# Splitting float64 weights into two float32r parts: a 24-bit conversion of five VectorE operations and one subtraction, in place of eight VectorE and two GpSimd operations

## The chip, the cores and the metric

The kernel runs on one core of one Trainium2 chip. The metric is device time in microseconds (us) of one execution. The core has a matmul engine (TensorE, PE in the profile, its weight loads PEld), VectorE (DVE), ScalarE (ACT), GpSimd (POOL) and SyncE (SP), which here issues all DMA transfers. Each engine works through its own list of instructions in order and waits only where an operand or a buffer is not ready.

## The reference

Clustered attention, then two feed-forward layers on its output:

```python
# attention: B, H, S, D = 2, 8, 768, 64; a key counts only in the query's cluster (16 clusters)
mask = q_assign[:, :, :, None] == k_assign[:, :, None, :]
scores = np.where(mask, scale * np.matmul(q, k.transpose(0, 1, 3, 2)), -1e9)
attn_out = np.matmul(softmax(scores), v)
x = attn_out.transpose(0, 2, 1, 3).reshape(B * S, H * D)      # 1536 x 512
# first layer: w_in 512 x 2048 and w_out 2048 x 512 are float64
r = np.maximum(x @ w_in, 0.0)
x = (r * r) @ w_out
# second layer: 4 experts, w1 512 x 1024 and w2 1024 x 512 each, float32
for e in range(4):
    out += p[:, e:e + 1] * (np.maximum(x @ w1[e], 0.0) @ w2[e])
```

`scale * (1 / sqrt(...))` makes the first layer's two weight matrices float64; every other input is float32.

## The kernel before, in words

A float32 value is carried as hi + lo, two float32r parts, so that three single-pass products (hi hi, hi lo, lo hi) add up to a float32 product. Every weight therefore has to be split on the chip into a hi and a lo tile before PE can use it.

**Attention** is a software pipeline over 96 units of 128 queries, a step each. `ORDER` writes out in which order the parts of an even and of an odd step are emitted: scores (`S`), row maximum on DVE (`M`, line 507), exponential on ACT (`E`, line 518), transposes (`T0`, `T1`) whose hi part ACT copies (`H`, line 536) and whose lo part DVE subtracts (`L`, line 537), products with v (`P`, lines 545 and 547) and their sum (`O`, line 563). The part `K`, in even steps from step 8 on, pops one item of the list `cq`: the conversion of the four blocks of the first layer's first weight chunk, and behind it the two loads of that chunk's `w_out` half.

**The first MoE layer** has 4 chunks of 512 hidden units, the second 8. Its work is a list `its` of (chunk, token block of 512, group of 128 hidden units), 12 per chunk. In slot n the program emits `gemm1(n)` (12 matmuls of 512 columns, lines 637 to 639), `gemm2(n - 4)` (12 matmuls, line 667) and then `run_plan(n)`, which emits what is due of weight loads and conversions. After `gemm1` of the first layer ACT runs relu, square and a copy to the hi part (lines 645 to 647, "the trio" below), and GpSimd subtracts for the lo part `hl` (line 648). After every fourth `gemm2` four accumulators `o` are emptied: by ACT copies for the first chunk (line 678), by DVE additions after it (line 680).

**The conversion** of a block (128 hidden units, a 128x512 tile) is `split64`. A float64 arrives as two 32-bit words. Before, it had three stages, a slot apart: shift and mask the high word (`f1` to `f4`, lines 153 to 169) and multiply by a 0/1 mask on GpSimd (line 170); copy to hi on ACT (line 174) and extract the remaining mantissa bits (lines 175 to 183, the subtraction on GpSimd); subtract hi (line 187) and add the remaining bits (line 190). `split_plan` puts the stages on slots, one block per slot: slots 0 to 19 and 24 to 31 start a block each (28 blocks), 4 more are converted in attention. `split32`, for the second layer, has one stage.

The scheduling is manual: each engine's order is the order in which the program is written.

Of the kernel before, what the change touches and what calls it, by code (L numbers as in the profile page):

```python
# [8 lines left out]
F32 = mybir.dt.float32  # L9
F32R = mybir.dt.float32r  # L10
I32 = mybir.dt.int32
AF = mybir.ActivationFunctionType
ALU = mybir.AluOpType
AX = mybir.AxisListType
PSUM = bass.MemoryType.PSUM

# A float32 value is carried as hi + lo, two float32r parts of 12 significant
# bits each, so that single-pass products of the parts add up to the float32
# product.  Inside an attention head, token p * 6 + t sits in column t * 128 + p.


# Order of the parts of a step of the attention pipeline, and the steps, counted
# from the first one of a head, at which its preparation is done.
ORDER = [
# [3 lines left out]
START = {'t': [1, 3, 3, 3], 'stack1': 6, 'stack': 7, 'head': [[1, 2, 3], [7, 8, 8]]}  # L28
FL = {"f7": "P", "chain": "V", "po": "V", "xh": "P", "xm": "P", "xl": "P", "kh": "P", "kl": "P", "vh": "P", "vl": "P", "f4": "V"}
AT = {"gap": 3, "stack1": -11, "stack": -9, "assign": -9, "oh0": -5, "oh1": -4, "splitv": -3,  # L30
# [4 lines left out]
def moe_attention_kernel(  # L35
# [13 lines left out]
    nc = tc.nc  # L49

    def eng(x):
        return {"V": nc.vector, "P": nc.gpsimd}[FL[x]]

# [8 lines left out]
    FC = 512  # L62
# [5 lines left out]
    scale = 1.0 / float(D) ** 0.5  # L68
# [17 lines left out]

# [1 line left out]
    # The first layer's weights are float64: a pair of 32-bit words each, the  # L88
    # upper one with the sign, the exponent and 20 mantissa bits.
    NC1 = moe_w_in.shape[1] // FC  # L90
# [33 lines left out]
    def w_block(ci, part, j):  # L124
        """hi and lo of the 128 hidden units j of a chunk: [128, 4, 128] or [128, 512]"""
        if (ci, part) not in w_t:
            w_t[ci, part] = tuple(
                w_pool[ci % 2, part].tile([128, 4, 512], F32R, tag=f"w{part}{x}", name=f"w{part}{x}")
                for x in "hl")
        hi, lo = w_t[ci, part]  # L130
        if part == 0:
            return hi[:, :, j * 128:(j + 1) * 128], lo[:, :, j * 128:(j + 1) * 128]
        return hi[:, j], lo[:, j]

    def split64(ci, part, j, cv):
        r = raw_t[ci, part, j // 2].bitcast(I32)
        jj = j % 2
        if part == 0:
            shp = [128, 4, 128]
            r = r.rearrange("p (k f w) -> p k f w", k=4, w=2)[:, :, jj * 128:(jj + 1) * 128]  # L140
            low, high = r[:, :, :, 0], r[:, :, :, 1]
        else:
            shp = [128, 512]
            r = r.rearrange("p (k f w) -> p k f w", k=2, w=2)[:, jj]
            low, high = r[:, :, 0], r[:, :, 1]
        st = {}

        def tile_(x):
            st[x] = cv.tile(shp, F32, tag="cv" + x, name="cv" + x)
            return st[x]  # L150

        def f1():
            nc.vector.tensor_scalar(  # L153
                tile_("a").bitcast(I32), high, 3, 0x3FFFFFF8,
                op0=ALU.logical_shift_left, op1=ALU.bitwise_and)

        def f2():
            nc.vector.tensor_scalar(  # L158
                tile_("b").bitcast(I32), high, 0x78000000, None, op0=ALU.bitwise_and)

        def f3():
            ai = st["a"].bitcast(I32)
            nc.vector.scalar_tensor_tensor(  # L163
                out=ai, in0=high, scalar=-0x40000000, in1=ai,
                op0=ALU.bitwise_and, op1=ALU.bitwise_or)

        def f4():
            e = eng("f4") if cv is cv_p[0] and len(cv_p) == 1 else nc.vector
            e.tensor_scalar(st["b"], st["b"], 2.0 ** -15, None, op0=ALU.is_ge)  # L169
            nc.gpsimd.tensor_tensor(st["a"], st["a"], st["b"], op=ALU.mult)  # L170

        def f5():
            st["hi"], st["lo"] = w_block(ci, part, j)
            nc.scalar.copy(st["hi"], st["a"])
            nc.vector.tensor_scalar(  # L175
                tile_("c").bitcast(I32), st["a"].bitcast(I32), -0x800000, None,
                op0=ALU.bitwise_and)

        def f6():
            nc.vector.scalar_tensor_tensor(  # L180
                out=tile_("d").bitcast(I32), in0=low, scalar=9, in1=st["c"].bitcast(I32),
                op0=ALU.logical_shift_right, op1=ALU.bitwise_or)
            nc.gpsimd.tensor_tensor(st["d"], st["d"], st["c"], op=ALU.subtract)

        def f7():
            e = eng("f7") if cv is cv_p[0] and len(cv_p) == 1 else nc.vector
            e.tensor_tensor(st["b"], st["a"], st["hi"].bitcast(F32), op=ALU.subtract)  # L187

        def f8():
            nc.vector.scalar_tensor_tensor(  # L190
                out=st["lo"], in0=st["d"], scalar=2.0 ** -20, in1=st["b"],
                op0=ALU.mult, op1=ALU.add)
        return [[f1, f2, f3, f4], [f5, f6], [f7, f8]]

# [10 lines left out]
    def split_plan(ci, part, j, slot):  # L205
        """the stages of a block, a slot apart: [(slot, order, f)]"""
        st = []

        def stage(k):
            if k == 0:  # L210
                st.extend((split64 if ci < NC1 else split32)(ci, part, j, cv_p[j % len(cv_p)]))
            for f in st[k]:
                f()
        return [(slot + k, -k, lambda k=k: stage(k)) for k in range(3 if ci < NC1 else 1)]

    # ================= attention =================
    with tc.manual_schedule():
# [22 lines left out]
        def load_pair(j):  # L240
            """k and q of heads 2j and 2j + 1, side by side"""
            b, h = divmod(2 * j, H)
# [20 lines left out]

# [1 line left out]
        c_sb = sm_p.tile([128, D], F32, tag="c_sb", name="c_sb", bufs=1)  # L265
# [13 lines left out]
        for c in range(C):  # L279
            nc.gpsimd.memset(wgt[:, :, c:c + 1], float(C - c))  # L280
        # sel[4 t + 2 h + s, t, 64 h + d] = 1: adds up 1 / sum (hi and lo) of a
        # token for the 64 rows of its head
        idv = identf[0:NTT * 4, 0:NTT * 4].rearrange("p (t h s) -> p t h s", t=NTT, h=2)
# [5 lines left out]

# [1 line left out]
        # q carries the softmax scale, a power of two, from here on.  # L291
        # Stacked along the contraction: [q hi; q hi] with [k hi; k lo], then
        # [q lo; one-hot cluster] with [k hi; -2^100 off its cluster], whose last
        # rows add 0 inside a cluster and -2^100 outside.
        vt, stk, kq, ohs, ohm = {}, {}, {}, {}, {}
# [14 lines left out]
        def double(i, nm):  # L310
            """k or q of a head, twice side by side"""
            t = nat[i, nm] = nat_p.tile([128, NTT, 2, D], F32, tag=nm, name=nm)
# [16 lines left out]
        def split_direct(i, nm, m):  # L329
            """the stacks of head i from its transposes on both partition halves"""  # L330
            def new(x, rows):
# [28 lines left out]
        def trans_slot(j, nm, half):  # L360
            """transpose k or q of a head pair and split it"""
            def f():
# [110 lines left out]
        def onehot_first():  # L473
            """the one-hot rows of head 0, without a detour over DMA"""
            for e, nm in ((1, "k2"), (0, "q2")):
# [11 lines left out]

# [1 line left out]
        s_ps, p_sb, nb_t, sums_t, pt_t, po_t, xs_t = {}, {}, {}, {}, {}, {}, {}  # L489
# [133 lines left out]

# [1 line left out]
        mp = {}  # L625
# [94 lines left out]

# [1 line left out]
        def warm_pe(n):  # L722
            """products of no use, that keep the clock of TensorE up"""
            w = ps_o.tile([128, 256], F32, tag="po", name="po")
# [10 lines left out]

# [1 line left out]
        csq = sm_p.tile([128, D], F32, tag="csq", name="csq", bufs=1)  # L737
# [69 lines left out]

        # what a step does besides its unit of queries
        early, slots = {}, {}
# [87 lines left out]

        # the last pair of units and the last heads, beside the first products of the MoE
        def early_gemm1(n):
# [22 lines left out]

# [1 line left out]
        dpv = dp.rearrange("p b t e -> p (b t) e")  # L924
# [7 lines left out]

# [1 line left out]
        for nm in ("w10", "w11", "acc"):  # L934
# [43 lines left out]
```

## Time and profile before

| | |
|---|---|
| median of 3 runs | 1134.59 us (1133.72, 1134.59, 1138.93) |
| profiled execution, from first to last instruction | 1132.6 us |
| PE busy | 1079.9 us (95%) |
| DVE busy | 618.4 us (55%) |
| ACT busy | 439.6 us (39%) |
| POOL busy | 397.9 us (35%) |
| PE mean granted clock | 0.980 |

The profiled execution is an execution of its own; its record gives the span, and the three runs lie 1.1, 2.0 and 6.3 us above that span. Busy times overlap, since the engines work side by side. A matmul's shown duration includes the pipeline's depth (0.39 us for one of 512 columns), so PE's pace is read from the distance between starts, or from the number of matmuls in a stretch of time. "Idle before" an instruction is the time its engine stood still ahead of it, and the arrow names what it waited for.

### The profile page before, as it was taken

The numbers are of one execution on the slowest core, as the hardware profiler recorded it, in microseconds if no ns is written. First come the engines' busy times: TensorE is split into PE (matmuls) and PEld (weight loads), VectorE is DVE, ScalarE is ACT, GpSimd is POOL, SyncE is SP. The second block draws the span as 40 slices with busy tenths as digits, with TensorE's granted clock in tenths as the row PEclk, the third lists the DMA queues.
The fourth block names the chain that finished last, engine by engine and source line by source line (L and its number), as shares of the span: only waits on it lengthen the run. The fifth ranks groups of instructions, "written<-read, shape, count | busy, mean of one in ns | idle before, by whom it ended". The sixth has DMA issues, their size and how long they took to land.

```text
span 1132.6 us, 14354 instructions
## 1 busy us (share of the span) xinstructions
PE 1079.9 (95%) x5502; PEld 910.1 (80%) x5502; DVE 618.4 (55%) x1014; ACT 439.6 (39%) x894; POOL 397.9 (35%) x364
## 2 busy tenths in 40 slices
PE   8799999999988887989999999999999999999998
PEld 7798888888866666878888888888888888888887
DVE  7799999999799999695012223223222222322322
ACT  5578887888733333333443112111111111111110
POOL 3346755553366666555445212020211102021000
PEclk9899999999998988999999999999999999999999
DMA  4565555663022221121110201011110201100011
GB/s 146 131 153 129 127 121 126 144 173 77 1 74 75 75 75 65 46 66 47 38 38 1 75 1 65 11 38 38 38 38 1 75 1 38 38 1 1 1 38 74
DMA packets 51812, 70.61 MB, mean 62 GB/s; under 512 B 25664, under 2 KB 28224, under 8 KB 51744
## 3 DMA queue, kind: packets, MB, share of 16 engines
q1 hardware_dynamic: 51744, 69.70, 21.9%
q8 instruction: 43, 0.70, 0.3%
q14 instruction: 25, 0.20, 0.1%
HBM read 43.05 MB, written 3.15 MB: 41 GB/s over the span
## 4 chain that ended last, share of the span: by engine, by line
PE 58%; DVE 14%; issue 0%; DVEq 0%
PE o L667 29%; PE h L637 9%; PE h L638 9%; PE h L639 9%; DVE cvb L158 3%; DVE cvc L175 2%; DVE w0l L190 2%; DVE cvd L180 1%; DVE cvb L187 1%; DVE w1l L190 1%; DVE cva L163 1%; DVE cva L153 1%; DVE cvb L169 1%; DVE acc L680 0%; DVE acc L692 0%
## 5 line engine op out<-in xcount | busy, mean ns | idle before, releaser
L651 DVE SCALAR_TENSOR_TENSOR hl<-h,hh 128x512 fp32r<-128x512 f32 x96 | 66.4, 692 | 393.4 <-ACT hh L650 393.4
L650 ACT ACTIVATE hh<-h 128x512 fp32r<-128x512 f32 x96 | 57.4, 598 | 429.0 <-PE h L639 429.0
L637 PE MATMUL h<-xh,w0h 128*128 128x512 f32 x560 | 218.4, 390 | 0.0
L638 PE MATMUL h<-xl,w0h 128*128 128x512 f32 x560 | 218.0, 389 | 0.0
L639 PE MATMUL h<-xh,w0l 128*128 128x512 f32 x560 | 217.9, 389 | 0.0
L667 PE MATMUL o<-w1h,hh 128*128 128x512 f32 x384 | 149.4, 389 | 0.0
L667 PE MATMUL o<-w1l,hh 128*128 128x512 f32 x384 | 149.4, 389 | 0.0
L667 PE MATMUL o<-w1h,hl 128*128 128x512 f32 x384 | 149.4, 389 | 0.0
L202 POOL TENSOR_TENSOR w0l<-raw,w0h 128x512 fp32r<-128x512 f32 x32 | 41.2, 1289 | 236.7 <-ACT w0h L201 236.7
L637 PEld LDWEIGHTS h<-xh,w0h 128*128 128x128 f32 x560 | 105.6, 189 | 22.0
L638 PEld LDWEIGHTS h<-xl,w0h 128*128 128x128 f32 x560 | 105.4, 188 | 22.1
L639 PEld LDWEIGHTS h<-xh,w0l 128*128 128x128 f32 x560 | 105.4, 188 | 21.9
L537 DVE TENSOR_TENSOR ptl<-t,pth 128x384 fp32r<-128x384 f32 x192 | 99.8, 548 | 8.4 <-ACT pth L536 7.7
L667 PE MATMUL o<-hh,w1h 128*128 128x512 f32 x192 | 79.9, 416 | 24.2 <-ACT acc L678 13.3
L531 PE MATMUL t<-identf,p 128*128 128x128 f32 x576 | 92.9, 284 | 7.4 <-DVE ptl L537 6.6
L507 DVE TENSOR_REDUCE nb<-s 128x1 f32<-128x768 f32 x96 | 91.0, 948 | 7.4 <-PE s L498 6.6
L536 ACT CAST pth<-t 128x384 fp32r<-128x384 f32 x192 | 83.9, 479 | 28.0 <-PE t L531 26.7
L648 POOL TENSOR_TENSOR hl<-r,hh 128x512 fp32r<-128x512 f32 x48 | 71.3, 1487 | 65.8 <-ACT hh L647 28.9
L518 ACT ACTIVATE p<-s,nb 128x768 f32<-128x768 f32 x96 | 86.7, 903 | 6.9 <-DVE nb L507 6.0
L498 PE MATMUL s<-k,q 80*128 80x384 f32 (+1 forms) x384 | 86.5, 347 | 0.2 <-DVE q L340 0.2
L667 PE MATMUL o<-hh,w1l 128*128 128x512 f32 x192 | 79.5, 414 | 5.0 <-DVE w1l L190 5.0
L667 PEld LDWEIGHTS o<-w1h,hh 128*128 128x128 f32 x384 | 72.1, 188 | 15.0
(147 smaller groups left out, 1842.2 us busy)
## 6 DMA issues: line engine op xcount, KB each, us to landing
raw<-in_moe_w_dram SPq DMA_DIRECT2D x16, 1024.0 KB, 5.0
raw<-in_moe_w_in_dram SPq DMA_DIRECT2D x8, 1024.0 KB, 5.2
raw<-in_moe_w_out_dram SPq DMA_DIRECT2D x8, 1024.0 KB, 4.9
q<-nqh SPq DMA_DIRECT2D x42, 192.0 KB, 3.0
k<-nkh SPq DMA_DIRECT2D x28, 192.0 KB, 3.7
q<-nql SPq DMA_DIRECT2D x28, 192.0 KB, 3.8
nv<-in_v_dram SPq DMA_DIRECT2D x16, 192.0 KB, 3.8
out_dram<-acc SPq DMA_DIRECT2D x12, 256.0 KB, 2.1
```

Of the source, the lines that this page charges most:

```text
L498: nc.tensor.matmul(s[:, j, 0:HALF], stk[i, nq][:, t * 128:(t + 1) * 128], stk[i, nk][:, j * HALF:(j + 1) * HALF], start=first, stop=not first)
L507: nc.vector.tensor_reduce(out=nb, in_=s_ps[u][:, :, 0:HALF], axis=AX.XY, op=ALU.max, negate=True)
L518: nc.scalar.activation(p, s_ps.pop(u)[:, :, 0:HALF], AF.Exp, bias=nb_t.pop(u), accum_out=sums_t[hp][:, i % 2, t:t + 1])
L531: nc.tensor.transpose(tp[:, j], p_sb[u][:, half, j * 128:(j + 1) * 128], identf)
L536: return (lambda: nc.scalar.copy(dh, tp), lambda: nc.vector.tensor_tensor(dl, tp, dh.bitcast(F32), op=ALU.subtract))
L537: lambda: nc.vector.tensor_tensor(dl, tp, dh.bitcast(F32), op=ALU.subtract))
L637: nc.tensor.matmul(ps, wh[:, kt, ms], xh[tb][:, kt], start=(kt == 0), stop=False)
L638: nc.tensor.matmul(ps, wh[:, kt, ms], xl[tb][:, kt], start=False, stop=False)
L639: nc.tensor.matmul(ps, wl[:, kt, ms], xh[tb][:, kt], start=False, stop=(kt == KD - 1))
L648: nc.gpsimd.tensor_tensor(hl, r, hh.bitcast(F32), op=ALU.subtract)
L651: nc.vector.scalar_tensor_tensor(out=hl, in0=ps, scalar=0.0, in1=hh.bitcast(F32), op0=ALU.max, op1=ALU.subtract)
L667: nc.tensor.matmul(o_t[n], a, b, start=(ft == 0 and z == 0), stop=(ft == NF - 1 and z == 2))
```

## The change

`split64` gets two stages. The first, on DVE alone, clears the sign of the high word, raises the value to at least 2^-15 (read as float32, in place of the 0/1 mask and its product), shifts, puts sign and top exponent bit back and adds three bits of the low word, so that one 32-bit float with 24 significant bits is left in `a`. The second copies `a` to hi on ACT and subtracts hi from `a`: on GpSimd while attention runs (`len(cv_p) == 1`), on DVE after it. The tiles `cvb`, `cvc` and `cvd` are gone. The list `cq` holds 3 items a block instead of 8, so attention's conversion is emitted in steps 8 to 34 instead of 8 to 74, and the two `w_out` loads come in steps 32 and 34 instead of 72 and 74.

```diff
-FL = {"f7": "P", "chain": "V", ..., "f4": "V"}
+FL = {"chain": "V", ...}
...
         def f1():
+            a = st["a"] = cv.tile(shp, F32, tag="cva", name="cva")
             nc.vector.tensor_scalar(
-                tile_("a").bitcast(I32), high, 3, 0x3FFFFFF8,
+                a.bitcast(I32), high, 0x7FFFFFFF, None, op0=ALU.bitwise_and)
+            nc.vector.tensor_scalar(a, a, 2.0 ** -15, None, op0=ALU.max)
+            nc.vector.tensor_scalar(
+                a.bitcast(I32), a.bitcast(I32), 3, 0x3FFFFFF8,
                 op0=ALU.logical_shift_left, op1=ALU.bitwise_and)
 
         def f2():
-            nc.vector.tensor_scalar(
-                tile_("b").bitcast(I32), high, 0x78000000, None, op0=ALU.bitwise_and)
-
-        def f3():
             ai = st["a"].bitcast(I32)
             nc.vector.scalar_tensor_tensor(
                 out=ai, in0=high, scalar=-0x40000000, in1=ai,
                 op0=ALU.bitwise_and, op1=ALU.bitwise_or)
-
-        def f4():
-            e = eng("f4") if cv is cv_p[0] and len(cv_p) == 1 else nc.vector
-            e.tensor_scalar(st["b"], st["b"], 2.0 ** -15, None, op0=ALU.is_ge)
-            nc.gpsimd.tensor_tensor(st["a"], st["a"], st["b"], op=ALU.mult)
-
-        def f5():
-            st["hi"], st["lo"] = w_block(ci, part, j)
-            nc.scalar.copy(st["hi"], st["a"])
-            nc.vector.tensor_scalar(
-                tile_("c").bitcast(I32), st["a"].bitcast(I32), -0x800000, None,
-                op0=ALU.bitwise_and)
-
-        def f6():
             nc.vector.scalar_tensor_tensor(
-                out=tile_("d").bitcast(I32), in0=low, scalar=9, in1=st["c"].bitcast(I32),
+                out=ai, in0=low, scalar=29, in1=ai,
                 op0=ALU.logical_shift_right, op1=ALU.bitwise_or)
-            nc.gpsimd.tensor_tensor(st["d"], st["d"], st["c"], op=ALU.subtract)
-
-        def f7():
-            e = eng("f7") if cv is cv_p[0] and len(cv_p) == 1 else nc.vector
-            e.tensor_tensor(st["b"], st["a"], st["hi"].bitcast(F32), op=ALU.subtract)
-
-        def f8():
-            nc.vector.scalar_tensor_tensor(
-                out=st["lo"], in0=st["d"], scalar=2.0 ** -20, in1=st["b"],
-                op0=ALU.mult, op1=ALU.add)
-        return [[f1, f2, f3, f4], [f5, f6], [f7, f8]]
+
+        def f3():
+            hi, lo = w_block(ci, part, j)
+            nc.scalar.copy(hi, st["a"])
+            e = nc.gpsimd if len(cv_p) == 1 else nc.vector
+            e.tensor_tensor(lo, st["a"], hi.bitcast(F32), op=ALU.subtract)
+        return [[f1, f2], [f3]]
...
-        return [(slot + k, -k, lambda k=k: stage(k)) for k in range(3 if ci < NC1 else 1)]
+        return [(slot + k, -k, lambda k=k: stage(k)) for k in range(2 if ci < NC1 else 1)]
```

The change's short description also speaks of the lo part of the squared relu tiles (`hl`) on VectorE; in the code that subtraction is the same GpSimd instruction in both kernels, line 648 before and line 629 after.

The order in which DVE has its instructions in the MoE slots, where a block of the first layer's weights is converted per slot (`w1l` is a lo tile of `w_out`). Before, one block after the other:

```order
496 L190 SCALAR_TENSOR_TENSOR w1l<-cvd,cvb 128x512
497 L175 TENSOR_SCALAR cvc<-cva 128x512
498 L180 SCALAR_TENSOR_TENSOR cvd<-raw,cvc 128x512
499 L153 TENSOR_SCALAR cva<-raw 128x512
500 L158 TENSOR_SCALAR cvb<-raw 128x512
501 L163 SCALAR_TENSOR_TENSOR cva<-raw,cva 128x512
502 L169 TENSOR_SCALAR cvb<-cvb 128x512
503 L187 TENSOR_TENSOR cvb<-cva,w1h 128x512
```

And after the change:

```order
488 L173 TENSOR_TENSOR w1l<-cva,w1h 128x512
489 L153 TENSOR_SCALAR cva<-raw 128x512
490 L155 TENSOR_SCALAR cva<-cva 128x512
491 L156 TENSOR_SCALAR cva<-cva 128x512
492 L162 SCALAR_TENSOR_TENSOR cva<-raw,cva 128x512
493 L165 SCALAR_TENSOR_TENSOR cva<-raw,cva 128x512
```

Eight instructions of a block, taken from three blocks in turn, became six, of which the five on `cva` are of one block and each read what the one before wrote.

GpSimd in the same slots, before (`hl` is the lo part of a squared relu tile):

```order
184 L183 TENSOR_TENSOR cvd<-cvd,cvc 128x512
185 L170 TENSOR_TENSOR cva<-cva,cvb 128x512
186 L648 TENSOR_TENSOR hl<-r,hh 128x512
187 L183 TENSOR_TENSOR cvd<-cvd,cvc 128x512
188 L170 TENSOR_TENSOR cva<-cva,cvb 128x512
```

And after the change, from the last instructions of attention (`rb`, `xh`, `xl` are its normalized outputs) to the second layer's first lo tile `w0l`:

```order
159 L584 TENSOR_TENSOR rb<-rb,xs 128x384
160 L596 TENSOR_TENSOR xh_79<-rb,zeros 128x384
161 L598 TENSOR_TENSOR xl_82<-rb,xh_79 128x384
162 L629 TENSOR_TENSOR hl<-r,hh 128x512 x37
163 L183 TENSOR_TENSOR w0l<-raw,w0h 128x4x128
```

Of three GpSimd instructions a slot one is left.

DVE in attention, at the step in which the conversion begins (`nb` is the row maximum of a unit, `ptl` the lo part of its transposes). Before:

```order
72 L537 TENSOR_TENSOR ptl<-t,pth 128x3x128 x2
73 L153 TENSOR_SCALAR cva<-raw 128x512
74 L507 TENSOR_REDUCE nb<-s 128x1
75 L409 TENSOR_REDUCE A<-m 128x192
76 L439 TENSOR_REDUCE mx<-A 128x12
```

And after the change:

```order
72 L518 TENSOR_TENSOR ptl<-t,pth 128x3x128 x2
73 L153 TENSOR_SCALAR cva<-raw 128x512
74 L155 TENSOR_SCALAR cva<-cva 128x512
75 L156 TENSOR_SCALAR cva<-cva 128x512
76 L488 TENSOR_REDUCE nb<-s 128x1
```

The row maximum now comes behind three operations of the conversion instead of one.

## Rows read from the trace of the kernel before

**Rows 1.** The overview, the span in 40 equal slices of 28.3 us: busy tenths of PE and of DVE.

```profile
PE   8799999999988887989999999999999999999998
...
DVE  7799999999799999695012223223222222322322
```

**Rows 2.** Windows, from 315 to 515 us and from 520 to 1120 us: length, busy us and number of instructions of PE, PEld, DVE, ACT and POOL, then the granted clock, the DMA share and GB/s.

```profile
315.00:515.00 200.00, 170.78 (x692) 137.36 (x691) 183.95 (x227) 73.24 (x125) 121.65 (x82) 0.92 0.21 69
520.00:1120.00 600.00, 600.00 (x2649) 496.99 (x2648) 143.48 (x212) 123.16 (x215) 117.95 (x92) 1.00 0.09 30
```

**Rows 3.** The waits of PE: who waited for what, us in total, how often, the longest.

```profile
PE o L667 <- ACT acc L678: 13.3, 3, 4.9
PE o L667 <- DVE acc L680: 10.9, 2, 7.1
...
PE o L667 <- DVE w1l L190: 5.0, 4, 2.4
```

**Rows 4.** Timeline of PE: start, duration, instruction, and in brackets the idle time before it and its releaser. A matmul that waited for the first block's `w1l`, and two behind a wait for an accumulator.

```profile
317.39 0.50 PE L667 MATMUL o<-hh,w1l 128*128 128x512 f32 x1 [1.87 <-DVE w1l L190]
...
406.71 0.63 PE L667 MATMUL o<-hh,w1l 128*128 128x512 f32 x1
407.13 0.63 PE L667 MATMUL o<-hl,w1h 128*128 128x512 f32 x1
```

**Rows 5.** Timeline of DVE over one slot, with the same columns.

```profile
359.17 1.59 DVE L190 SCALAR_TENSOR_TENSOR w0l<-cvd,cvb 128x512 fp32r<-128x512 f32 x1
360.69 1.52 DVE L175 TENSOR_SCALAR cvc<-cva 128x512 int32<-128x512 int32 x1
362.25 0.69 DVE L180 SCALAR_TENSOR_TENSOR cvd<-raw,cvc 128x512 int32<-128x512 int32 x1
362.85 0.42 DVE L153 TENSOR_SCALAR cva<-raw 128x512 int32<-128x512 int32 x1
363.19 1.52 DVE L158 TENSOR_SCALAR cvb<-raw 128x512 int32<-128x512 int32 x1
364.63 0.68 DVE L163 SCALAR_TENSOR_TENSOR cva<-raw,cva 128x512 int32<-128x512 int32 x1
365.24 0.41 DVE L169 TENSOR_SCALAR cvb<-cvb 128x512 f32<-128x512 f32 x1
365.57 0.68 DVE L187 TENSOR_TENSOR cvb<-cva,w0h 128x512 f32<-128x512 f32 x1
366.35 1.59 DVE L190 SCALAR_TENSOR_TENSOR w0l<-cvd,cvb 128x512 fp32r<-128x512 f32 x1
```

**Rows 6.** Timeline of POOL over the same slot.

```profile
358.61 1.60 POOL L170 TENSOR_TENSOR cva<-cva,cvb 128x512 f32<-128x512 f32 x1 [1.37 <-DVE cvb L169]
360.18 1.75 POOL L648 TENSOR_TENSOR hl<-r,hh 128x512 fp32r<-128x512 f32 x1
363.08 1.35 POOL L183 TENSOR_TENSOR cvd<-cvd,cvc 128x512 f32<-128x512 f32 x1 [1.16 <-DVE cvd L180]
```

**Rows 7.** Timeline of ACT over the same slot: the hi copy of a block, then the trio.

```profile
360.25 0.62 ACT L174 CAST w0h<-cva 128x512 fp32r<-128x512 f32 x1 [4.74 <-POOL cva L170]
360.78 0.59 ACT L645 ACTIVATE r<-h 128x512 f32<-128x512 f32 x1
361.40 0.64 ACT L646 ACTIVATE r<-r 128x512 f32<-128x512 f32 x1
362.07 0.62 ACT L647 CAST hh<-r 128x512 fp32r<-128x512 f32 x1
```

**Rows 8.** Groups of instructions by line and shape over the whole span: count, busy us, mean ns of one, idle us before and its releasers. The accumulator additions of the first layer.

```profile
L680 DVE TENSOR_TENSOR acc<-o,acc 128x512 f32<-128x512 f32 x36 | 23.7, 687 | 65.5 <-PE o L667 65.4
```

**Rows 9.** The same view of DVE from 50 to 240 us, the stretch of attention in which the first half of the first chunk is converted.

```profile
L163 DVE SCALAR_TENSOR_TENSOR cva<-raw,cva 128x512 int32<-128x512 int32 x4 | 2.7, 681 | 0.0
L190 DVE SCALAR_TENSOR_TENSOR w0l<-cvd,cvb 128x512 fp32r<-128x512 f32 x4 | 2.7, 663 | 0.0
L180 DVE SCALAR_TENSOR_TENSOR cvd<-raw,cvc 128x512 int32<-128x512 int32 x4 | 2.7, 663 | 0.0
...
L175 DVE TENSOR_SCALAR cvc<-cva 128x512 int32<-128x512 int32 x4 | 2.3, 565 | 0.0
L158 DVE TENSOR_SCALAR cvb<-raw 128x512 int32<-128x512 int32 x4 | 2.2, 560 | 0.0
L153 DVE TENSOR_SCALAR cva<-raw 128x512 int32<-128x512 int32 x4 | 1.7, 415 | 0.0
L169 DVE TENSOR_SCALAR cvb<-cvb 128x512 f32<-128x512 f32 x4 | 1.5, 387 | 0.0
```

**Rows 10.** The window of that stretch, columns as in Rows 2.

```profile
50.00:240.00 190.00, 181.84 (x1332) 163.35 (x1332) 181.04 (x365) 151.44 (x356) 111.01 (x119) 0.98 0.57 135
```

**Rows 11.** Timeline of DVE at the end of attention (columns as in Rows 4).

```profile
299.65 0.42 DVE L153 TENSOR_SCALAR cva<-raw 128x512 int32<-128x512 int32 x1
299.99 0.42 DVE L158 TENSOR_SCALAR cvb<-raw 128x512 int32<-128x512 int32 x1
...
303.28 0.43 DVE L563 TENSOR_TENSOR xs<-po,tmp 64x256 f32<-64x256 f32 x1 [1.93 <-ACT tmp L561]
...
310.73 0.56 DVE L617 TENSOR_TENSOR xl<-rb,xh 128x384 fp32r<-128x384 f32 x1 [0.58 <-ACT xh L613]
311.21 0.42 DVE L175 TENSOR_SCALAR cvc<-cva 128x512 int32<-128x512 int32 x1
```

More of the change, by code (lines that the diff above doesn't have):

```diff
@@ L28 @@
 START = {'t': [1, 3, 3, 3], 'stack1': 6, 'stack': 7, 'head': [[1, 2, 3], [7, 8, 8]]}
-FL = {"f7": "P", "chain": "V", "po": "V", "xh": "P", "xm": "P", "xl": "P", "kh": "P", "kl": "P", "vh": "P", "vl": "P", "f4": "V"}
+FL = {"chain": "V", "po": "V", "xh": "P", "xm": "P", "xl": "P", "kh": "P", "kl": "P", "vh": "P", "vl": "P"}
 AT = {"gap": 3, "stack1": -11, "stack": -9, "assign": -9, "oh0": -5, "oh1": -4, "splitv": -3,
@@ L146, in split64 @@
         st = {}
-        def tile_(x):
-            st[x] = cv.tile(shp, F32, tag="cv" + x, name="cv" + x)
-            return st[x]
         def f1():
+            a = st["a"] = cv.tile(shp, F32, tag="cva", name="cva")
             nc.vector.tensor_scalar(
-                tile_("a").bitcast(I32), high, 3, 0x3FFFFFF8,
+                a.bitcast(I32), high, 0x7FFFFFFF, None, op0=ALU.bitwise_and)
+            nc.vector.tensor_scalar(a, a, 2.0 ** -15, None, op0=ALU.max)
+            nc.vector.tensor_scalar(
+                a.bitcast(I32), a.bitcast(I32), 3, 0x3FFFFFF8,
                 op0=ALU.logical_shift_left, op1=ALU.bitwise_and)
         def f2():
-            nc.vector.tensor_scalar(
-                tile_("b").bitcast(I32), high, 0x78000000, None, op0=ALU.bitwise_and)
-        def f3():
             ai = st["a"].bitcast(I32)
```

## The prediction, made before the change was run

> **What bounds the kernel now.** I read the 40-slice overview first: which engine is full where. Up to slice 10 TensorE (PE) and VectorE (DVE) are both near full; in slices 12 to 19 PE has holes (7, 8) and DVE mostly stands at 9; from slice 20 on PE is full and DVE nearly empty [rows 1]. So three stages: attention (0 to about 300 us), the first MoE layer while weights are converted (about 315 to 515), the rest.
>
> Then the windows. From 520 to 1120 us PE runs 2649 matmuls in 600 us, 0.2265 us each, at a granted clock of 1.00: full rate. From 315 to 515 us it runs 692 in 200 us; at full rate these take 692 x 0.2265 = 156.7 us, so this stage **loses 43.3 us** [rows 2]. DVE is busy for 184 of its 200 us, the clock is 0.92.
>
> PE's waits show where: behind ScalarE's (ACT) `acc` copies 13.3 us in 3 waits, behind DVE's `acc` adds 10.9 in 2, behind DVE's `w1l` 5.0 in 4, together 29.2 [rows 3]. [...]
>
> Why are accumulators late? A slot (one gemm1 and one gemm2 of 12 matmuls) is 24 x 0.2265 = 5.44 us of PE. The DVE timeline shows one converted block from `w0l` at 359.17 to the next at 366.35: **7.18 us**, eight operations back to back with no idle [rows 5]. Three of the eight are long: L190 1.59, L175 1.52, L158 1.52, where the same operations, undisturbed, take 0.66, 0.42 and 0.42 [rows 9, 11]. Each overlaps a GpSimd (POOL) operation and ends 0.3 to 0.55 us after it: L170 runs 358.61 to 360.21, L190 ends 360.76; L648 ends 361.93, L175 362.21; L183 ends 364.43, L158 364.71 [rows 5, 6]. POOL's work is thus paid on DVE, 0.9 + 1.1 + 1.1 = 3.1 us of the 7.18. ACT's copy of the hi part stood idle 4.74 us for POOL's `cva`, and the squared-relu trio queues behind it [rows 7]; that is how the late block reaches the `acc` copies.
>
> [...]
>
> **The change, part by part.**
>
> *MoE conversion, DVE.* Removed per block: L153, L158, L163, L169, L175, L180, L187, L190. Added: mask 0.42 (as L158 undisturbed), max 0.41 (as L169), shift-and-mask 0.42 (as L153), two scalar_tensor_tensor 0.68 and 0.69 (as L163, L180), one subtraction 0.68 (as L187) [rows 5, 11]: 3.30 us. Now each operation reads what the one before wrote. The one such pair in the timeline, L175 then L180, has 362.25 - 362.21 = 0.04 us between them [rows 5]: 5 gaps, 0.2. Sum 3.5 us.
>
> *POOL.* L170 and L183 go; only `hl` (L648) is left, so at most one collision a slot, 1.1 us: 4.6 us. From the second chunk on four `acc` adds of 0.687 us come every fourth slot [rows 8], 0.7 a slot: **5.3 us at most against PE's 5.44**. In the slot with the adds DVE has 4.6 + 2.75 = 7.35, 1.9 over; the three others spare 0.84 each, and the adds are queued ahead of that slot's conversion, so the accumulators are freed in time.
>
> *ACT.* Still one hi copy a block, 0.62, now waiting on DVE's chain instead of POOL. In PE's rhythm, counted from the end of a gemm1: trio to 1.9, hi copy to 2.5 [rows 7]; the subtraction stretched by `hl` to 3.9; five operations to 6.7; ACT's next hi copy comes at 5.44 + 1.9 = 7.3. There is 0.6 us to spare, so nothing waits.
>
> *Start.* The four `w1l` waits (5.0) [rows 3] came of three stages and a clogged POOL; the lo part now takes two stages, so the lo part of block 0 can follow `xl` (310.73 + 0.56) and is ready by about 312.0 [rows 11]; PE wants it at 317.39 - 1.87 = 315.5 [rows 4]. The longer first chain (2.8 us from 299.65) ends before `xs` at 303.28, where DVE idled 1.93 us anyway [rows 11].
>
> So PE sets the pace, without long waits its clock stays up, and nearly all of 43.3 us comes back. I take **-42**, leaving 1.3 for a short wait or two like the two smaller `w1l` ones.
>
> *Attention.* Converting chunk 0's first part takes 2.7 + 2.7 + 2.7 + 2.3 + 2.2 + 1.7 + 1.5 = 15.8 us of DVE today [rows 9]; the new five cost 4 x 2.62 = 10.5, with gaps about 11: 5 us fewer. POOL loses 8 operations, but is not the bound there (busy 111 of 190 us). DVE is busy 181.0 and PE 181.8 [rows 10], so neither alone sets the time. Best case all 5 us; worst case the bursts hurt: two or three operations now go into one step (1.3 us where one of 0.4 to 0.7 stood), 8 bursts x 0.7 = 5.6 us less some relief from the 20 steps left free, and the first mask of a block now waits for POOL's subtraction two steps earlier. Bounds -5 and +5; I take **-2**: with both engines equally full, somewhat under half of DVE's relief should show.
>
> *Free of cost.* The two `w_out` loads move on SP's queue from steps 72 and 74 to 32 and 34; their buffers are read out by then, and the stack transfers behind them are issued at least 9 units ahead of their use, some 27 us (96 units in about 300 us), which covers a wait behind a load. The `hl` subtraction, which the short description sends to VectorE, stays on GpSimd in the code: 0.
>
> Sum: -42 - 2 = -44 from the profiled span of 1132.6 us: 1088.6. The median of the runs lies 2.0 above that span (1134.6; the runs are 1133.7 to 1138.9): **1090.6 us**.
>
> **Rivals.**
>
> *DVE still sets some slots.* If every collision lasts its full 1.1 us where the adds fall, the five waits for accumulators [rows 3] stay at 1 to 2 us with 2.4 us of slow clock each: 5 x 3.5 = 17, about 1107; with half of them 1099. For it: 5.3 against 5.44 is thin. Against: the adds read PSUM and one SBUF operand, are not stretched in the trace (0.687 on average [rows 8]), and are queued early. 14%.
>
> *Attention loses from bursts.* +5 instead of -2: about 1098. For: PE and DVE both at 95%. Against: less work in sum on both DVE and POOL. 6%.
>
> [...] 3%. [...]
>
> *Slower: the ACT to DVE hand-off closes into a loop.* DVE's subtraction waits for the hi copy, the next hi copy for DVE's chain, and the trio queues behind that copy. Once PE has to wait for the trio, the slot is hi 0.62 + subtraction behind `hl` 1.6 + chain 2.8 + trio 1.9 = 6.9, and with the four `acc` copies of a fourth slot (0.6 each, as the trio's) 9.3; if gaps or a second collision add 0.5 a slot, the mean is 6.9 + 0.6 + 0.5 = 8.0, over 7.18: +0.8 in 28 slots, +22, about 1157. It decides when the chain ends over 0.6 us later than reckoned, four slots running (PE runs four slots ahead). For: ACT did wait 4.74 us a slot [rows 7]. Against: POOL's two operations have left that path. 3%.
>
> *The change does not do what it says*: `hl` stays. On DVE it would cost 0.68 and remove the collision of 1.1, so the time would be the same; no chance of its own.
>
> **How the numbers follow.** Forecast 74%: 1086 to 1098 (attention -5 to +3, MoE -43.3 to -40); 1 us lower for the spread of the runs. The first rival is taken in up to 1107, the second wholly. Outside lie 1119, 1157 and a gain beyond the bounds, together under 2 in 10: range **1085 to 1107**. A difference under 0.5% (5.7 us) cannot be told from no change here; all cases but the loop lie below 1129, and I keep 0.03 for a sum of mishaps between: faster 0.94, same 0.03, slower 0.03.
>
> **What would show it.** Right: from 315 us on PE runs 24 matmuls per 5.44 us at clock 1.00 with no `acc` wait; the block cycle on DVE falls to 5.44 with idle in it; one stretched Vector operation a block. `w1l` waits vanish; attention ends 0 to 5 us earlier. Wrong: PE still waits for `acc`, or DVE stays at 9 tenths in slices 12 to 18, or gaps of over 0.1 us between the new dependent operations.

## The result, and the profile after

The changed kernel takes 1105.33 us (median of 4 runs, 1102.88 to 1106.55) against 1134.15 before: ratio 0.9743, 95% interval [0.9712, 0.9773]. The forecast was 1090.6, the range 1085 to 1107; the direction holds, and 14.7 us of the expected 43.6 are missing. The profiled execution spans 1100.8 us, 31.8 less than before.

The overview of the changed kernel, busy tenths of PE and DVE in 40 slices of 27.5 us, against [rows 1]:

```profile
PE   7887989999999999999999999999999999999998
...
DVE  8799979999978884741012322222222223222322
```

The holes of slices 12 to 19 are gone, and DVE is at 8 or less there. New holes stand in slices 3, 4 and 6, in the first half of attention. The windows say the same (length, busy us and count of PE, PEld, DVE, ACT and POOL, granted clock, DMA share, GB/s):

```profile
315.00:515.00 200.00, 197.81 (x873) 163.27 (x872) 127.08 (x190) 93.69 (x159) 52.18 (x40) 1.00 0.22 74
...
50.00:240.00 190.00, 173.67 (x1266) 157.86 (x1266) 172.19 (x336) 144.22 (x335) 90.76 (x103) 0.96 0.56 133
```

From 315 to 515 us PE ran 692 matmuls before, at a clock of 0.92 [rows 2]; now 873, close to 200 / 0.2265 = 883, at 1.00. (The stage begins some 9 us later than before, so a few of attention's smaller matmuls are among them.) From 50 to 240 us PE and DVE are both less busy than before [rows 10], 173.7 and 172.2 where 181.8 and 181.0 stood, and the clock is 0.96 instead of 0.98: there attention waits. PE's waits answer to [rows 3]; of the long waits for accumulators and `w1l` one of 2.2 us is left, and waits of attention have come:

```profile
PE t L512 <- DVE ptl L518: 11.2, 13, 3.3
PE m L350 <- ACT kqf L357: 5.4, 3, 4.1
...
PE o L648 <- ACT acc L659: 2.2, 1, 2.2
```

How late attention is can be read from the row maxima, one for each of the 96 units (line 507 before, 488 after). Units 13, 36, 37, 38 and 95, counted from 0, in the timeline of DVE before:

```profile
64.24 0.95 DVE L507 TENSOR_REDUCE nb<-s 128x1 f32<-128x768 f32 x1
...
129.59 0.96 DVE L507 TENSOR_REDUCE nb<-s 128x1 f32<-128x768 f32 x1
...
133.11 0.94 DVE L507 TENSOR_REDUCE nb<-s 128x1 f32<-128x768 f32 x1
...
136.37 0.96 DVE L507 TENSOR_REDUCE nb<-s 128x1 f32<-128x768 f32 x1
...
292.48 0.96 DVE L507 TENSOR_REDUCE nb<-s 128x1 f32<-128x768 f32 x1
```

and after the change:

```profile
63.35 0.94 DVE L488 TENSOR_REDUCE nb<-s 128x1 f32<-128x768 f32 x1
...
139.01 0.96 DVE L488 TENSOR_REDUCE nb<-s 128x1 f32<-128x768 f32 x1
...
141.24 0.95 DVE L488 TENSOR_REDUCE nb<-s 128x1 f32<-128x768 f32 x1
...
148.96 0.96 DVE L488 TENSOR_REDUCE nb<-s 128x1 f32<-128x768 f32 x1
...
301.81 0.96 DVE L488 TENSOR_REDUCE nb<-s 128x1 f32<-128x768 f32 x1
```

The lag is -0.9 us at unit 13, +9.4 at unit 36, +8.1 at 37, +12.6 at 38 and +9.3 at the end. So attention lost 10.3 us between units 13 and 36, 4.5 in a single jump at unit 38, and got some 4 back behind it. The first 13 units are left out: kernels with the same instructions there lie some 3 us apart (-0.9 here, +2.3 in run 3 below), so a cost of the first conversion steps can't be read. From unit 14 on the reading is steady: in runs 1 and 7, which leave attention as it was, the lag stays within 0.2 us to the end. The rest of the program gained 31.8 + 9.3 = **41.1 us**.

The conversion steps with two or three VectorE operations, "bursts" from here on, are steps 8 to 28, two per block; six of the eight lie between units 13 and 36. The windows of these units, before and after, with the columns of [rows 2]:

```profile
64.24:129.59 65.35, 63.76 (x479) 57.39 (x478) 63.26 (x131) 54.06 (x128) 37.49 (x41) 1.00 0.58 132
...
63.35:139.01 75.66, 65.43 (x461) 58.25 (x462) 69.98 (x135) 54.05 (x125) 36.54 (x40) 0.95 0.49 113
```

DVE was busy for 97% of this stretch already. It now has 6.7 us more work there, since 15 conversion operations fall on these units instead of 10 and some operations are longer, and it stands idle 3.6 us more. Together these are the 10.3 us.

**One step of attention.** DVE from unit 24 to unit 25 before:

```profile
95.35 0.96 DVE L507 TENSOR_REDUCE nb<-s 128x1 f32<-128x768 f32 x1
...
98.13 0.68 DVE L190 SCALAR_TENSOR_TENSOR w0l<-cvd,cvb 128x512 fp32r<-128x512 f32 x1
98.73 0.95 DVE L507 TENSOR_REDUCE nb<-s 128x1 f32<-128x768 f32 x1
```

and in the changed kernel, with POOL, ACT and PE in the same place:

```profile
99.48 0.96 DVE L488 TENSOR_REDUCE nb<-s 128x1 f32<-128x768 f32 x1
...
102.23 1.31 DVE L162 SCALAR_TENSOR_TENSOR cva<-raw,cva 128x512 int32<-128x512 int32 x1
103.57 1.37 DVE L165 SCALAR_TENSOR_TENSOR cva<-raw,cva 128x512 int32<-128x512 int32 x1
104.87 0.94 DVE L488 TENSOR_REDUCE nb<-s 128x1 f32<-128x768 f32 x1
```

```profile
102.15 0.84 POOL L361 TENSOR_TENSOR nqh<-kqf,zeros 128x384 fp32r<-128x384 f32 x1
103.07 1.33 POOL L363 TENSOR_TENSOR nql<-kqf,nqh 128x384 fp32r<-128x384 f32 x1
```

```profile
105.85 0.90 ACT L499 ACTIVATE p<-s,nb 128x768 f32<-128x768 f32 x1 [1.97 <-DVE nb L488]
```

```profile
107.29 0.55 PE L512 MATMUL t<-identf,p 128*128 128x128 f32 x3 [3.31 <-DVE ptl L518]
```

Two conversion operations, each stretched from 0.69 to over 1.3 behind a GpSimd operation, stand ahead of the row maximum for 2.6 us, where one stood there for 0.6 before. The lag grows from 4.1 us (99.48 - 95.35) to 6.1 (104.87 - 98.73). ACT's exponential waits 1.97 us for it, and the transposes wait 3.31 for what should have freed their buffer.

At the other five bursts behind unit 13 the lag grows in the same way, by 2.2 us at the other stretched one and by 1.1, 1.0, 1.1 and 0.7 at the four that ran at their free length. The six make 8.2 of the 10.3 us; the rest comes in the units between them.

**The jump at unit 38.** SP's issues in the changed kernel (start, duration, transfer), then POOL, ACT and PE:

```profile
134.72 0.53 SPq L110 DMA_DIRECT2D raw<-in_moe_w_out_dram  x1
...
136.57 0.55 SPq L375 DMA_DIRECT2D k<-nkh  x1
```

```profile
144.13 0.83 POOL L361 TENSOR_TENSOR nkh<-kqf,zeros 128x384 fp32r<-128x384 f32 x1 [6.74 <-DMA k<-nkh]
```

```profile
146.06 0.49 ACT L357 ACTIVATE kqf<-m 128x384 f32<-128x384 f32 x1 [4.80 <-POOL nkl L363]
```

```profile
146.60 0.90 PE L350 MATMUL m<-identf,nq 128*128 128x128 f32 x3 [4.13 <-ACT kqf L357]
```

The copy of `nkh` to a stack is issued 1.9 us behind a 1 MB weight load and lands after 7.3 us, where such copies take 3.9 in the median; from 134 to 146 us the DMA engines are busy for 0.89 of the time. By the prediction's estimate the stack is not needed for some 27 us, but the source tile `nkh` is: POOL has to write the next pair's values into it and waits 6.74 us for the copy to have read it, ACT waits for POOL, PE for ACT.

**A slot of the MoE**, answering to [rows 5]: DVE of the changed kernel, and the hi copy on ACT [rows 7].

```profile
382.38 0.69 DVE L173 TENSOR_TENSOR w0l<-cva,w0h 128x512 fp32r<-128x512 f32 x1 [0.69 <-ACT w0h L171]
382.99 0.42 DVE L153 TENSOR_SCALAR cva<-raw 128x512 int32<-128x512 int32 x1
383.44 0.43 DVE L155 TENSOR_SCALAR cva<-cva 128x512 f32<-128x512 f32 x1
383.90 0.43 DVE L156 TENSOR_SCALAR cva<-cva 128x512 int32<-128x512 int32 x1
384.37 1.77 DVE L162 SCALAR_TENSOR_TENSOR cva<-raw,cva 128x512 int32<-128x512 int32 x1
386.17 0.69 DVE L165 SCALAR_TENSOR_TENSOR cva<-raw,cva 128x512 int32<-128x512 int32 x1
387.55 0.69 DVE L173 TENSOR_TENSOR w0l<-cva,w0h 128x512 fp32r<-128x512 f32 x1 [0.69 <-ACT w0h L171]
```

```profile
386.90 0.62 ACT L171 CAST w0h<-cva 128x512 fp32r<-128x512 f32 x1 [2.73 <-DVE cva L165]
```

A block takes 387.55 - 382.38 = 5.17 us where it took 7.18, with one stretched operation (L162, 1.08 us over its free 0.69) and gaps of 0.03 or 0.04 us along the chain.

### The profile page after: what moved, and what is told of

It is laid out like the page before. It is cut to its first block, busy times and chain, and to the rows that moved or that the text cites. A ratio compares the mean times of both kernels' runs of the same rounds, so it can differ in the third digit from the quotient of the medians.

```text
span 1100.8 us, 14190 instructions
## 1 busy us (share of the span) xinstructions
PE 1066.0 (97%) x5502; PEld 903.7 (82%) x5502; DVE 546.6 (50%) x950; ACT 441.5 (40%) x894; POOL 297.1 (27%) x300
## 4 chain that ended last, share of the span: by engine, by line
PE 84%; DVE 11%; ACT 2%; DMA 1%; issue 1%; POOL 1%; SPq 0%; POOLq 0%; DVEq 0%
PE o L648 34%; PE h L620 11%; PE h L618 11%; PE h L619 11%; PE t L512 4%; PE s L479 4%; DVE ptl L518 2%; PE po L526 2%; PE po L528 2%; PE m L384 1%; DVE nb L488 1%; DVE cva L162 1%; DVE cva L165 1%; DMA k<-nkh 1%; PE m L577 1%
## 5 line engine op out<-in xcount | busy, mean ns | idle before, releaser
L629 POOL TENSOR_TENSOR hl<-r,hh 128x512 fp32r<-128x512 f32 x48 | 63.1, 1314 | 184.3 <-ACT hh L628 127.5
L518 DVE TENSOR_TENSOR ptl<-t,pth 128x384 fp32r<-128x384 f32 x192 | 100.2, 548 | 14.9 <-ACT pth L517 13.9
L488 DVE TENSOR_REDUCE nb<-s 128x1 f32<-128x768 f32 x96 | 90.9, 947 | 10.2 <-PE s L479 9.5
L499 ACT ACTIVATE p<-s,nb 128x768 f32<-128x768 f32 x96 | 86.8, 904 | 10.3 <-DVE nb L488 9.7
L512 PEld LDWEIGHTS t<-identf,p 128*128 128x128 f32 x576 | 65.6, 144 | 27.1 <-DVE ptl L518 24.2
L648 PEld LDWEIGHTS o<-w1l,hh 128*128 128x128 f32 x384 | 72.1, 188 | 15.0
L648 PEld LDWEIGHTS o<-w1h,hl 128*128 128x128 f32 x384 | 72.1, 188 | 15.0
```

What stands on the lines that cost most here:

```text
L488: nc.vector.tensor_reduce(out=nb, in_=s_ps[u][:, :, 0:HALF], axis=AX.XY, op=ALU.max, negate=True)
L499: nc.scalar.activation(p, s_ps.pop(u)[:, :, 0:HALF], AF.Exp, bias=nb_t.pop(u), accum_out=sums_t[hp][:, i % 2, t:t + 1])
L512: nc.tensor.transpose(tp[:, j], p_sb[u][:, half, j * 128:(j + 1) * 128], identf)
L518: lambda: nc.vector.tensor_tensor(dl, tp, dh.bitcast(F32), op=ALU.subtract))
L629: nc.gpsimd.tensor_tensor(hl, r, hh.bitcast(F32), op=ALU.subtract)
L648: nc.tensor.matmul(o_t[n], a, b, start=(ft == 0 and z == 0), stop=(ft == NF - 1 and z == 2))
```

## The experiments

Two theories of the missing gain: **A**, the MoE gained what was forecast, and attention lost about 9 us, to conversion operations in a row and to two loads that came at a bad place; **B**, in each run, another cause for the same step. Each was timed against the kernel before on the same chip (1133.0 to 1133.9 us); "the lag" is that of the row maxima, as above.

**1. Old conversion in attention, new one in the MoE** (`old_attn`).

```diff
-            cq += [f for fs in split64(0, 0, j, cv_p[0]) for f in fs]
+            cq += [f for fs in split64_old(0, 0, j, cv_p[0]) for f in fs]
```

> New conversion in the MoE slots, the old one (eight steps a block, loads in steps 72 and 74) in attention. Theory A (the MoE gained what was forecast, about 41 us, and attention lost 9 us of it): the last row maximum of attention is back at about 292.5 us and the time is 1134.2 - 41 = 1093 to 1097. Rival B (the 9 us were not lost in attention's conversion, but by another placement of tiles or by the run itself): the time stays at 1104 to 1106.

1093.69 us, ratio 0.9658 [0.9617, 0.9699]; the lag is -1.5 at unit 13 and -1.4 at the end. A holds: the loss is attention's conversion, together with the two loads that follow it in the list.

**2. New conversion in attention, old one in the MoE** (`old_moe`), the same edit the other way round.

> The old conversion in the MoE slots, the new one in attention, with the early loads. Theory A (the two parts of the change add up): 1134.2 + 9.3 = about 1143, slower than before. Rival B (attention's delay is made up at its end, or was not caused by the new conversion): 1132 to 1136.

1147.69 us, ratio 1.0121 [1.0084, 1.0158], slower than before. The lag grows from 3.9 at unit 13 to 13.9 at unit 36 and is 14.9 at the end, all of it in the span (1147.6). A holds. Of the 4.7 us over the expectation 3.9 lie, in the profiled execution, in the first 13 units, which differ between executions; why all four runs (1145.4 to 1149.4) lie above 1143 is not shown.

**3. Loads moved back** (`late_loads`).

```diff
+        cq += [lambda: None] * (32 - len(cq))
         for n, x in enumerate(w_loads(0)[2:]):
             cq.append(lambda x=x: load_w(*x))
```

> The changed kernel with its two w_out loads moved back from steps 32 and 34 to steps 72 and 74. Theory A (two loads of 1 MB right in front of the loads of the next k and q hold the transfers up, which made the jump of 4.4 us between the row maxima 37 and 38): the jump is gone, 1105.3 - 4.4 = about 1101. Rival B (the jump belongs to the backlog of the conversion): 1105, with the jump still there.

1100.16 us, ratio 0.9694 [0.9653, 0.9734]. The lag is 11.4 at unit 37 and 11.9 at unit 38: no jump. A holds.

**4. One operation per step, loads late** (`fine_late`): the diff of run 3, and `f1` and `f2` cut up.

```diff
-        return [[f1, f2], [f3]]
+        return [[f1, f1b, f1c, f2, f2b], [f3]]
```

> As the run with late loads, and in attention each of the five VectorE operations has a step of its own (24 items in steps 8 to 54 instead of 12 in steps 8 to 30). Theory A (it was two or three operations in a row, in front of the next row maximum, that held each step up): nearly all of attention's loss goes, 1091 to 1096. Rival B (the work packed into fewer steps is what costs, however it is cut): about half of the 10 us of steps 8 to 34 stays, 1098 to 1101.

1090.28 us, ratio 0.9623 [0.9584, 0.9662]. Units 13 and 36 in DVE's timeline of this kernel:

```profile
60.82 0.94 DVE L497 TENSOR_REDUCE nb<-s 128x1 f32<-128x768 f32 x1
...
125.93 0.96 DVE L497 TENSOR_REDUCE nb<-s 128x1 f32<-128x768 f32 x1
```

They are 65.1 us apart, as before (65.35), where the changed kernel has 75.7. So the loss of these units is gone, as A expected, and B's half of it did not stay. But the run does not decide between the two causes: with one operation a step the conversion also takes twice as many steps, and only 10 operations fall on these units, as before. DVE's work there is back as well:

```profile
60.82:125.93 65.11, 62.32 (x469) 56.14 (x468) 62.51 (x129) 52.88 (x126) 34.26 (x39) 1.00 0.56 130
```

Whether the pieces were too long or the units held too much work for an engine that was 97% busy, no run tells apart. A run with one operation in every step, odd and even, would.

**5. One operation per step, loads right behind** (`fine`), in steps 56 and 58: run 4 without the padding.

> The changed kernel with one VectorE operation per step in attention, the loads right behind, in steps 56 and 58; these stand at the same place of the 12-step period of a head pair as steps 32 and 34, while 72 and 74 do not. Theory A (it is this place, right ahead of the copies of k and q to the stacks, that makes the jump): a jump of about 4 us again, now near unit 62, and 1090.3 + 4 = 1094. Rival B (the loads only hurt while attention is behind): no jump, 1089 to 1091.

1094.81 us, ratio 0.9648 [0.9628, 0.9668]. The lag is -3.8 at unit 61 and +0.7 at unit 62: the jump of 4.5 is back, though attention is not behind, and POOL waits for the same copy:

```profile
201.52 0.82 POOL L370 TENSOR_TENSOR nkh<-kqf,zeros 128x384 fp32r<-128x384 f32 x1 [6.40 <-DMA k<-nkh]
```

The kernel before and the changed kernel, with the loads elsewhere, have 1.77 and 2.05 us at this place. So it is the place in the head pair's period that hurts, as A has it.

**6. Old operations, two per step** (`old_pairs`): nothing of the change, only bundled.

```diff
-            cq += [f for fs in split64(0, 0, j, cv_p[0]) for f in fs]
+            fl = [f for fs in split64(0, 0, j, cv_p[0]) for f in fs]
+            cq += [lambda x=x, y=y: (x(), y()) for x, y in zip(fl[::2], fl[1::2])]
+        cq += [lambda: None] * (32 - len(cq))
```

> The kernel before, with the old conversion in attention issued two functions per step (16 items in steps 8 to 38) and the loads where they were, in steps 72 and 74. The same operations, only bundled. Theory A (two or more conversion operations in a row in one step hold up the next row maximum): attention loses about 5 to 8 us in steps 8 to 38 and gets back 2 to 4 by the free steps behind, 1136 to 1139. Rival B (what hurt was the new chain, each operation waiting for the one before in place): no loss, 1131 to 1134.

1142.26 us, ratio 1.0083 [1.0059, 1.0107]. From unit 13 to 36 the lag grows from 4.9 to 15.0, by 10.2, nearly as in the changed kernel (10.3). That the two agree so well is in part chance. Each block's last pair puts `f8` on DVE right behind `f7` on POOL, and in two blocks DVE stands waiting for it, a wait that the new conversion does not have:

```profile
107.20 1.30 DVE L190 SCALAR_TENSOR_TENSOR w0l<-cvd,cvb 128x512 fp32r<-128x512 f32 x1 [1.18 <-POOL cvb L187]
...
134.31 0.69 DVE L190 SCALAR_TENSOR_TENSOR w0l<-cvd,cvb 128x512 fp32r<-128x512 f32 x1 [2.21 <-POOL cvb L187]
```

Up to 3.4 of the 10.2 us belong to these waits. The 6.8 that are left lie within the 5 to 8 expected, and B, which expected no loss, is out: the in-place chain is not the cause. Like run 4 this one changes the pieces and the work in each step together.

**7. GpSimd's part of the MoE conversion on VectorE** (`all_dve`), in the kernel before.

```diff
-            nc.gpsimd.tensor_tensor(st["a"], st["a"], st["b"], op=ALU.mult)
+            (nc.gpsimd if len(cv_p) == 1 else nc.vector).tensor_tensor(
+                st["a"], st["a"], st["b"], op=ALU.mult)
```

and the same for the subtraction of line 183.

> The kernel before, with its two GpSimd operations of a MoE block's conversion (the product of line 170, the subtraction of line 183) issued on VectorE; attention as before. VectorE, which set the pace, gets two operations more. Theory A (each GpSimd operation was paid in full on VectorE through waiting): a block is 5.8 us of operations less some overlap, plus at most one wait of 1.1 behind hl, about 6.6 us instead of 7.18, times 28 slots: 16 us faster, 1117 against 1133. Rival B (the three long VectorE operations are long by themselves, by their kind): 7.18 + 1.4 = 8.6 us a block, about 40 us slower, 1170.

1124.73 us, ratio 0.9921 [0.9904, 0.9939]: faster by 9, with 1.4 us a block more on the engine that sets the pace. Timeline of DVE, and of POOL beside it:

```profile
363.81 1.52 DVE L153 TENSOR_SCALAR cva<-raw 128x512 int32<-128x512 int32 x1
365.25 0.41 DVE L158 TENSOR_SCALAR cvb<-raw 128x512 int32<-128x512 int32 x1
...
370.43 1.52 DVE L153 TENSOR_SCALAR cva<-raw 128x512 int32<-128x512 int32 x1
```

```profile
363.38 1.66 POOL L650 TENSOR_TENSOR hl<-r,hh 128x512 fp32r<-128x512 f32 x1 [4.89 <-ACT hh L649]
```

L158 (the mask), 1.52 in [rows 5] beside a GpSimd operation, is 0.41 without one; L153, 0.42 there, is now the one beside `hl` and takes 1.52. Length follows the neighbour, not the operation: on the block, which takes 6.62 us as expected, A holds, and B is out. On the time A expected too much: the gain is 9.4 us of span instead of 16, and 2.2 of it come from the first 13 units of attention; in the first slots PE now waits 3.2 us for `w1h` and 4.1 for `w1l`, and once 8.6 for an accumulator. How the difference divides among these was not taken apart.

**8. `hl` on VectorE** (`hl_dve`), as the change's short description says, in the changed kernel.

```diff
-                nc.gpsimd.tensor_tensor(hl, r, hh.bitcast(F32), op=ALU.subtract)
+                nc.vector.tensor_tensor(hl, r, hh.bitcast(F32), op=ALU.subtract)
```

> The changed kernel with the lo part of the squared relu tiles on VectorE too, as the change's short description has it. Theory A (PE sets the pace of the MoE slots either way; 0.7 us of work more on VectorE against a wait of up to 1.1 us less): within 2 us of the changed kernel, 1103 to 1107. Rival B (VectorE was still close to the bound): 3 us or more in either direction, with acc waits appearing or the one of 2.2 us gone.

1104.29 us, ratio 0.9738 [0.9724, 0.9753], the changed kernel's own within its interval. In the profiled execution two things cancel: the last wait for an accumulator is gone (the MoE gains 30.3 + 13.1 = 43.4 us, where the five traces with the changed kernel's MoE slots have 39.5 to 41.1), and the lag at attention's end happens to be 13.1 instead of 9.3, 2.6 of the difference from the first 13 units. So A on the time, B on the wait.

**9. All together** (`fine_late_hl`): runs 4 and 8.

> The three findings together: the new conversion, one VectorE operation per step in attention, the loads in steps 72 and 74, and the lo part of the squared relu tiles on VectorE. Theory A (they add up: 1090.3 with the single operations and late loads, less the 2.2 us wait for an accumulator, which was gone with hl on VectorE): 1087 to 1089, the fastest of all. Rival B (with 0.7 us more per slot VectorE is late again, now that the MoE starts earlier): 1090 or more.

1087.56 us (1087.08 to 1090.73), ratio 0.9595 [0.9573, 0.9617], faster than both kernels and as A expected. Its interval overlaps that of run 4 (0.9584 to 0.9662), so what `hl` on DVE adds to run 4 is not shown by the times; in the trace the MoE gains 43.4 us again, as in run 8. No wait for an accumulator or a weight is left among PE's waits, and PE is busy 98% of the span.

## Why the prediction was right in one part and wrong in the other

*What bounds the MoE slots, and the MoE conversion: right.* -42 forecast, -41.1 measured (39.5 to 41.1 in the five traces with the same MoE slots). The wait of a Vector operation behind a GpSimd one was priced at 1.1 us and is 1.08 (L162); run 7 shows it directly (L158, 0.41 us with no GpSimd operation beside it, 1.52 beside one in [rows 5]). The chain's gaps were taken as 0.04 us and are 0.02 to 0.04 between the five operations, over the 28 blocks of the MoE slots.

*ACT and DVE: too optimistic, without harm.* "0.6 us to spare, so nothing waits" was wrong in form: the loop of the slower rival does close while the late start is made up, subtraction, chain, hi copy, subtraction, with ACT waiting 2.73 us and DVE 0.69 in each turn. It is 5.17 us long, 0.27 under PE's 5.44, where that rival had 6.9 to 8.0. The rival priced the trio inside the loop; in the trace it runs beside the chain. One wait of 2.2 us is left, for the first accumulator; the forecast had left 1.3 for short waits and named "no `acc` wait" as a sign of being right.

*Start: right.* No `w1l` wait is left.

*Attention, -2 with bounds of -5 and +5: this step failed; it is +9.3.* Two of its sentences did.

- "8 bursts x 0.7 = 5.6 us", and "somewhat under half of DVE's relief should show": the price of a burst was taken as what it adds to one operation, and the relief from a sum over 190 us. Between units 13 and 36, where six of the bursts lie, DVE had next to no idle time, and there its work rose by 6.7 us. 10.3 us are lost, 1.7 a burst: in the trace the operations of the six sum to 10.1 us, of which 3 blocks x 2.62 = 7.9 is free length and 2.2 stretching behind GpSimd, in two bursts that add 2.2 and 2.0 to the lag where the other four add 0.7 to 1.1. One operation a step, over twice as many steps, costs no more than the old conversion did (run 4). How the price divides between the length of a piece and the work in a step stays open.
- "*Free of cost.* The two `w_out` loads ... which covers a wait behind a load": the cover was named for the stack that is written. What was late is the tile that is read: the next owner of `nkh` waits for the copy to have left it. 4.5 us, in one jump (runs 3 and 5).

The relief is there, but only once the conversion is over, where the old one still had an operation in every second step: some 4 us from unit 40 to the end, too little to pay for both. As a rival, attention's loss was named, at +5 and 6%; its mechanism was right for the bursts and its size half. The first rival, DVE setting some slots, which carried the range up to 1107, did not happen; the time falls into that part of the range for another reason, and that it lies inside is luck. Its sum takes 2.4 us of slow clock for each wait, an estimate, (43.3 - 29.2) / 6 from [rows 2] and [rows 3], that no run shows. What the traces show is a granted clock of 0.53 to 0.72 over the 5.5 to 6.1 us behind each of the six waits of 2.37 us and more in the kernel before, which is 1.7 to 2.8 us lost (length times what the clock lacks to 1.00), and of 1.00 over the 5.5 us from the start of the matmul that had waited 2.2 us in the changed kernel. The 1119 outside the range is a case of longer gaps between dependent operations, held at 3%; no run shows such gaps, the traces have 0.02 to 0.04 us.

*The change does not do what it says: right.* `hl` stays on GpSimd; run 8 shows what it would have brought, the last accumulator wait.

## What to carry to other kernels

In a step pipeline with no idle engine, ask not only how much work a change takes off an engine in sum, but how much it puts into each step, and in how long a piece, ahead of the step's critical operation: the new conversion has less work on DVE than the old one, yet it cost 10 us with two and three operations to a step, and nothing over the old one with one to a step over twice as many steps. When a transfer is moved, look at who waits for its neighbours' sources to be released (6.74 us here) as well as for their destinations. And time that a Vector operation gains or loses may belong to GpSimd: in run 7 moving GpSimd's work onto the bottleneck engine made the kernel faster by 9 us (1124.73 against 1133.88).

## What the runs showed of the hardware that had not been expected

The wait behind GpSimd hit more kinds of conversion operation than the three read before the change, also the two-input ones on integers (L162: 0.69 free, 1.77 beside `hl`), and also where GpSimd worked on quite different tiles (1.31 and 1.37 beside `nqh` and `nql`). A weight load of 1 MB (`w_out`) that lands in 4.9 us in the median took 9.7 when it was issued among the stack copies and the loads of the next keys and values, in the window from 138 to 152 us, where the DMA engines were busy for 0.98 of the time. And the granted clock of PE fell in attention too: behind the wait of 3.31 us above it was 0.50 from 110 to 112 us, and it is 0.91 in the windows 60 to 80, 100 to 120 and 140 to 160 us of the changed kernel, against 1.00 in the same windows before. What that adds to the price of a burst was not taken apart.
